# Two attention and MLP layers at one token, 8 rows: key scores of the next row moved ahead of a row's end, norms folded behind the projections, output projection as rows, PSUM banks by purpose

## Chip, cores, metric

One core of one Trainium2 chip runs the whole program. The metric is device time in microseconds (us). "PE" is the tensor engine, "DVE" the vector engine, "ACT" the scalar engine, "POOL" GpSimd, "SP" the engine whose queue issues the loads. PSUM is the memory that PE's products land in, divided into banks; HBM is the main memory that the loads read. The profiler also gives the "granted clock": the share of its full clock that PE was allowed. Rows are counted from 1 in the text.

## The reference, cut to what matters

```python
B, Sq, D = 8, 1, 448;  Hq, Hkv, Sk, Dh = 16, 8, 4096, 256;  F = 1792
def A(x):                        # attention, one query token per row
    q = x @ wq                   # 2 query heads share a key/value head
    p = softmax(q @ k_cache.T * Dh**-0.5)
    return (p @ v_cache) @ wo
def M(x):                        # with one token the shifted half of the mixer is zero
    return x + gelu(layernorm(x) @ w3) @ w4
x = x + A(layernorm(x));  x = x + M(layernorm(x))     # layer 1
x = x + A(layernorm(x));  x = x + M(layernorm(x))     # layer 2, same caches and weights
```

Each row's key or value cache of one head is 2 MB. Both layers read the same caches, so what stays on the chip between a row's layer 1 and its layer 2 need not be loaded twice. Layer 2's queries depend on everything that layer 1 did to that row.

## The kernel before

The kernel holds 30 slots of 512 KB (a quarter of one head's keys or values). Between the layers of a row it keeps the keys of five heads (20 slots) and half of one head's values (2 slots). Three "free heads" keep nothing. A list scheduler written in Python ("the planner") gives every engine a fixed order when the program is built; the loads go through one queue in program order and each waits until its slots are free.

A row ends with a *chain*: x1 (the row after layer 1's attention), a norm, the MLP, x2, a norm, the queries of layer 2, and then the first layer-2 scores. Only those scores free the 20 kept key slots. So from the last layer-1 head until then, the loads have 8 slots to live on.

The chain's norm, cut:

```python
def norm(src, skey, n, second):
    # mean: 4 matmuls with ones;  xc = src - mean;  sq = xc*xc
    pe(mean_mm, 4, ...);  dv(xc ...);  dv(sq ...)
    def var_mm(t):                       # f32 products
        for kc in range(4):
            last = t.matmul(psC[:, 8:8 + n], ones_f[0:k, :], sq[0:k, kc, 0:n], ...)
    pe(var_mm, 16, ...)
    # ... variance, two Newton steps, all on DVE ...
    dv(yb = xc * rstd * mask)            # ahead of the projection

def mlp(src, ...):
    norm(src, skey, n, True)
    pe(h_mm, 56, rd=YB + [...])          # needs yb
    # ... gelu ...
    pe(y_mm, 70, ...)
```

A head, cut. Its scores and its value products share one PSUM bank; two such banks take turns:

```python
def pair(layer, b, h, ...):
    ps, bk = psS[g % 2], ("S", g % 2)
    ks.update(load(A_k_cache, b, h, fresh))
    # per quarter: 8 transposes of 128x128 f32, then 16 score products of 48 columns
    if u not in keep_k: free_slots.append(ks[u])
    # max, exp -> pT, sum
    def back():                          # runs after the next head's scores
        vs.update(load(A_v_cache, b, h, fresh_v))
        # per quarter 8 value products, four column groups; each frees its slot
        # ...
        def wo_mm(t):                    # 20 matmuls per head
            for mt in range(NC5):
                for k in range(4):
                    last = t.matmul(psW[:, mt * YW:(mt + 1) * YW], dup(wo_sb, ...),
                                    bcast(oT[nr][:, c, j:j + 1], YW, 1), ...)
        pe(wo_mm, 20, ...);  dv(acc += psW)
```

The order of the heads:

```python
for b in range(B):
    mid(b, order2[:QFIRST])                    # the chain; QFIRST = 8 query groups
    layer1(b + 1, free_heads[:NFILL])          # NFILL = 2 whole heads beside the chain
    layer2(b, l2_heads[:2])
    layer1(b + 1, free_heads[NFILL:])
    layer2(b, l2_heads[2:])
    layer2(b, free_heads)
    layer1(b + 1, kept_heads)
```

## Time and profile before

| | before |
|---|---|
| median of 3 runs | 1180.18 us (1179.01 to 1184.13) |
| profiled span | 1175.4 us |
| read from HBM | 455.15 MB |
| PE busy | 1002.4 us (85%) |
| x1 to the first layer-2 score | 19.4 us in most rows |

The page of the kernel before, in part: busy time by engine, the rate in 40 equal slices, the instruction queue, HBM bytes, the engines' shares of the chain of work that ended last, and the group of the output projection (busy us, mean ns of one, idle time before it and what ended that).

```profile
span 1175.4 us, 45862 instructions
...
PE 1002.4 (85%) x21205; PEld 858.9 (73%) x21205; DVE 529.1 (45%) x1653; ACT 263.2 (22%) x826; POOL 97.9 (8%) x270
...
GB/s 341 408 420 394 343 415 423 418 402 339 392 422 419 391 374 411 425 415 330 388 423 422 414 354 399 425 418 411 348 396 425 418 396 358 414 413 363 343 424 154
...
q8 instruction: 166, 2.72, 0.9%
...
HBM read 455.15 MB, written 0.01 MB: 387 GB/s over the span
...
PE 61%; DMA 28%; issue 6%; DVE 5%; ACT 0%; POOL 0%; SPq 0%; POOLq 0%
...
L809 PE MATMUL psW<-oT,wo_sb 128*128 128x24 bf16 x2560 | 89.6, 183 | 5.7 <-DVE oT L799 3.3
```

Read the rate line as a heartbeat: the program is bound by its loads at about 420 GB/s, and roughly every fifth slice, once per row, it falls to 330 to 374.

Windows of 5 us around the end of row 2 of the kernel before (columns: busy us of each engine with its instructions, the granted clock, the DMA share, GB/s):

```profile
core 0: us, PE busy (x) PEld busy (x) DVE busy (x) ACT busy (x) POOL busy (x), PEclk, DMA share, GB/s
255.00:260.00 5.00, 4.08 (x34) 3.21 (x33) 1.61 (x4) 0.58 (x1) 0.00 (x0) 0.72 1.03 406
260.00:265.00 5.00, 5.00 (x100) 4.94 (x99) 3.32 (x13) 1.09 (x2) 0.00 (x0) 0.94 0.94 344
265.00:270.00 5.00, 5.00 (x125) 4.97 (x123) 3.47 (x13) 2.40 (x8) 0.75 (x2) 1.00 0.90 299
270.00:275.00 5.00, 5.00 (x142) 4.36 (x139) 2.27 (x8) 0.80 (x2) 0.00 (x0) 1.00 0.75 249
275.00:280.00 5.00, 4.79 (x100) 3.62 (x99) 3.23 (x19) 0.65 (x4) 0.75 (x2) 1.00 0.85 264
280.00:285.00 5.00, 4.29 (x153) 3.83 (x151) 2.03 (x10) 0.65 (x4) 0.75 (x2) 1.00 0.99 397
```

During the dip PE has no idle time left, and DMA does. Who keeps the loads waiting is in the waits of the DMA queue of the kernel before (us waited in total, times, longest):

```profile
SPq L444 <- PE psS L771: 475.2, 148, 11.7
SPq L444 <- PE psS L731: 448.1, 129, 12.3
```

L771 is the value products and L731 the scores: a load waits for PE to be done with the slot. Most of these waits cost nothing, since the queue issues far ahead of the engines that move the data; those at a row's end do.

The timeline of the kernel before, same row (start us, length us, engine, line, what it does):

```profile
260.70 0.17 DVE L821 TENSOR_TENSOR x1T<-acc,psW 128x5 bf16<-128x5 f32 x1
...
262.76 1.12 PE L568 MATMUL psC<-sq,ones_f 128*128 128x1 f32 x8
...
264.70 1.94 PE L838 MATMUL psT<-ident_f,kv 128*128 128x128 f32 x16
...
272.27 2.02 PE L674 MATMUL psC<-hT,w_sb 128*128 128x24 bf16 x70
...
277.89 0.70 PE L809 MATMUL psW<-oT,wo_sb 128*128 128x24 bf16 x20
...
280.26 0.96 PE L731 MATMUL psS<-q2T,kv 128*128 128x48 bf16 x32
```

x1 is there at 260.9 and the first layer-2 score starts at 280.3. In between the chain shares PE with transposes (L838), output projection (L809) and the rest of two whole heads of the next row.

### The profile page before, as it was taken

Reading aid. Unit: us, or ns where it says so; the run is one execution under the profiler, and the core shown is the slowest. Engines: PE = TensorE matmul, PEld = TensorE weight load, DVE = VectorE, ACT = ScalarE, POOL = GpSimd, SP = SyncE. Lnnn points to the kernel's source line nnn. Section 1 sums busy time; section 2 is a strip of 40 time slices with the busy share of each in tenths; the row PEclk is TensorE's granted clock in tenths of the full one; section 3 lists DMA queues with packets and bytes.
Section 4 is the critical chain, followed back from the end, with each engine's and each line's share of the span. In section 5 each row is a group of like instructions: output and inputs, shape, how many; then the busy total and the mean of one; then the engine's idle time right before and its main releaser. Section 6 shows DMA issues by size and latency. Waiting matters only on the chain.

```text
span 1175.4 us, 45862 instructions
## 1 busy us (share of the span) xinstructions
PE 1002.4 (85%) x21205; PEld 858.9 (73%) x21205; DVE 529.1 (45%) x1653; ACT 263.2 (22%) x826; POOL 97.9 (8%) x270
## 2 busy tenths in 40 slices
PE   4886988888898998888878898888978988889887
PEld 4775877777787776777767777776857877677775
DVE  3342534544354533555335543454435543354444
ACT  1221212221222211232122311222112321132111
POOL 0100001001100001000010100000010000110100
PEclk9898979998898988999889998899989998899988
DMA  9999999999999999999999999999999999999993
GB/s 341 408 420 394 343 415 423 418 402 339 392 422 419 391 374 411 425 415 330 388 423 422 414 354 399 425 418 411 348 396 425 418 396 358 414 413 363 343 424 154
DMA packets 62046, 458.10 MB, mean 390 GB/s; under 512 B 6288, under 2 KB 12320, under 8 KB 30240
## 3 DMA queue, kind: packets, MB, share of 16 engines
q1 hardware_dynamic: 61856, 455.19, 95.8%
q8 instruction: 166, 2.72, 0.9%
q14 instruction: 24, 0.20, 0.0%
HBM read 455.15 MB, written 0.01 MB: 387 GB/s over the span
## 4 chain that ended last, share of the span: by engine, by line
PE 61%; DMA 28%; issue 6%; DVE 5%; ACT 0%; POOL 0%; SPq 0%; POOLq 0%
PE psT L838 22%; DMA kv<-in_A_k_cache_dram 17%; PE psS L731 16%; DMA kv<-in_A_v_cache_dram 11%; PE psS L771 9%; PE psW L809 4%; PE psC L628 2%; PE psT L977 2%; DVE oS L783 2%; DVE oS L785 2%; PE psC L568 1%; PE psS L793 1%; PE psC L674 1%; PE psC L650 1%; DVE oT L799 0%
## 5 line engine op out<-in xcount | busy, mean ns | idle before, releaser
L838 PE MATMUL psT<-ident_f,kv 128*128 128x128 f32 x2816 | 390.5, 289 | 9.5 <-DMA kv<-in_A_k_cache_dram 9.2
L846 DVE COPY kv<-psT 128x512 f32<-128x512 f32 x400 | 275.3, 691 | 162.3 <-PE psT L838 158.8
L838 PEld LDWEIGHTS psT<-ident_f,kv 128*128 128x128 f32 x2816 | 326.8, 148 | 22.6 <-DMA kv<-in_A_k_cache_dram 15.6
L847 ACT COPY kv<-psT 128x512 f32<-128x512 f32 x304 | 178.2, 587 | 462.5 <-PE psT L838 462.3
L771 PE MATMUL psS<-kv,pT 128*2 128x256 bf16 x4096 | 173.8, 289 | 37.0 <-DMA kv<-in_A_v_cache_dram 22.3
L752 ACT ACTIVATE pT<-psS,nb 128x32 bf16<-128x32 f32 x256 | 72.9, 295 | 416.9 <-DVE nb L746 416.9
L731 PE MATMUL psS<-q2T,kv 128*128 128x48 bf16 x4096 | 143.0, 190 | 21.3 <-issue 20.3
L731 PEld LDWEIGHTS psS<-q2T,kv 128*128 128x128 bf16 x4096 | 131.3, 101 | 29.1 <-issue 27.7
L731 PE MATMUL psS<-q1T,kv 128*128 128x48 bf16 x4096 | 142.8, 184 | 2.8 <-issue 1.9
L731 PEld LDWEIGHTS psS<-q1T,kv 128*128 128x128 bf16 x4096 | 129.7, 97 | 21.2 <-issue 15.6
L771 PEld LDWEIGHTS psS<-kv,pT 128*2 128x2 bf16 x4096 | 77.7, 85 | 74.9 <-issue 26.5
L744 POOL PARTITION_ALL_REDUCE gm<-pm x128 | 45.4, 355 | 893.2 <-DVE pm L742 770.7
L742 DVE TENSOR_REDUCE pm<-psS 128x2 f32<-128x64 f32 x128 | 28.7, 225 | 156.7 <-PE psS L731 156.1
L809 PEld LDWEIGHTS psW<-oT,wo_sb 128*128 128x128 bf16 x2560 | 80.3, 97 | 21.4 <-DVE oT L799 14.4
L809 PE MATMUL psW<-oT,wo_sb 128*128 128x24 bf16 x2560 | 89.6, 183 | 5.7 <-DVE oT L799 3.3
L783 DVE CAST oS<-psS 128x256 bf16<-128x256 f32 x128 | 54.3, 424 | 87.8 <-PE psS L771 85.0
L793 PEld LDWEIGHTS psS<-sel,oS 128*128 128x128 bf16 x512 | 24.7, 98 | 90.6 <-DVE oS L785 88.6
L793 PE MATMUL psS<-sel,oS 128*128 128x2 bf16 x512 | 32.3, 167 | 67.0 <-DVE oS L785 66.5
L977 PE MATMUL psT<-ident_b 128*128 128x256 bf16 x518 | 85.6, 285 | 1.8 <-issue 1.8
L757 POOL PARTITION_ALL_REDUCE Db<-rs x128 | 51.3, 401 | 154.4 <-ACT pT L752 154.4
L785 DVE TENSOR_TENSOR oS<-psS,oS 128x256 bf16<-128x256 f32 x128 | 54.3, 424 | 2.9
L977 PEld LDWEIGHTS psT<-ident_b 128*128 128x128 bf16 x518 | 40.8, 100 | 16.1 <-issue 12.0
(83 smaller groups left out, 475.4 us busy)
## 6 DMA issues: line engine op xcount, KB each, us to landing
kv<-in_A_v_cache_dram SPq DMA_DIRECT2D x64, 2048.0 KB, 16.6
kv<-in_A_k_cache_dram SPq DMA_DIRECT2D x48, 2048.0 KB, 22.4
kv<-in_A_v_cache_dram SPq DMA_DIRECT2D x86, 1024.0 KB, 19.7
kv<-in_A_k_cache_dram SPq DMA_DIRECT2D x46, 1024.0 KB, 25.6
kv<-in_A_v_cache_dram SPq DMA_DIRECT2D x68, 512.0 KB, 7.4
kv<-in_A_k_cache_dram SPq DMA_DIRECT2D x68, 512.0 KB, 11.6
wo_sb<-in_A_wo_dram SPq DMA_DIRECT2D x1, 3584.0 KB, 46.2
wq_sb<-in_A_wq_dram SPq DMA_DIRECT2D x3, 1024.0 KB, 16.6
```

The costliest lines, as they stand in the source:

```text
L731: last = t.matmul(ps[:, 2 * i:2 * i + 2 * REP], a[:, c:256:2], bcast(rhs(c), REP, 1), start=(c == 0), stop=(c == 1))
L752: return a.activation(pT[nr][:, :, :].rearrange("p i j -> p j i")[:, jj, :], sview[:, jj, :], ACT.Exp, bias=nb[nr][:, jj:jj + 1], scale=IN ...
L757: plan.op("pool", lambda gp: gp.partition_all_reduce(Db[nr][:, :], rs[nr][:, :], P, RO.add), 0.5, "sum", rd=[("rs", nr, 0), ("rs", nr, 1)] ...
L771: last = t.matmul(ps[g4:g4 + 2, PV0:PV0 + DH], pT[nr][:, i, :], slot_ap(q, s * 256, 256), start=(i < 4), stop=(i >= 28), skip_group_check= ...
L783: plan.op("dve", lambda v: v.tensor_copy(oS[:, 0, :], po), 0.36, "o", rd=[("pv", par, x) for x in range(4)], wr=["oS0"], banks=[bk], prio=hi)
L785: plan.op("dve", lambda v: v.tensor_tensor(oS[:, 1, :], po, oS[:, 0, :], ALU.subtract), 0.36, "o", rd=["oS0"] + [("pv", par, x) for x in r ...
L793: last = t.matmul(ps[:, PV1 + 2 * c:PV1 + 2 * c + 2], oS[:, w, c * P:(c + 1) * P], sel[:, :], start=(w == 0), stop=(w == 1))
L809: last = t.matmul(psW[:, mt * YW:(mt + 1) * YW], dup(wo_sb, 2 * (2 * h + j) + c, mt), bcast(oT[nr][:, c, j:j + 1], YW, 1), start=(k == 0), ...
L838: last = t.transpose(psT[bank][:, s * P:(s + 1) * P], src, ident_f[:, :])
L846: return e.tensor_copy(dst, psT[bank][:, :])
L847: return e.copy(dst, psT[bank][:, :])
L977: last = t.matmul(psT[bank][:, 256 * i:256 * i + 256], ident_b[:, :], bcast(ident_b[:, :], 2, 1), start=True, stop=True)
```

## The change

Five things at once. (1) A head is split into a front (keys, scores, exponentials) and a back (values and what follows). The fronts of the next row's three free heads run *ahead* of the row's end, mixed with the kept heads; only their backs stay beside the chain. (2) Norms are folded behind the projections: the raw x goes through the weights while the moments are worked out, and a column sum of the weights corrects the result. (3) The output projection is 4 matmuls of 448 columns per head in four column groups, summed over seven heads in a PSUM bank; then two evacuations and a 10-matmul "turn"; the last head goes directly. (4) PSUM banks by purpose: one for scores, one for values, one for the chain, two for the rows, three instead of four for transposes. (5) The planner models PE's instruction fetches, and a filler (a matmul without use for the result, meant to keep PE's granted clock up) is one product of 512 columns rather than two of 256.

```diff
-LAG = 1
-QFIRST = 8
-NFILL = 2
+AHEAD = 1
+KSTEP = 2
+QFIRST = 1
+NFILL = 3
 ...
-    NT = 4
-    psS = [nc.alloc_psum_tensor(f"psS{i}", [P, 512], f32) for i in range(2)]
-    psC = nc.alloc_psum_tensor("psC", [P, 512], f32)
-    psW = nc.alloc_psum_tensor("psW", [P, 512], f32)
+    NT = 3 if LAY == "A" else 4                        # LAY = "A"
+    psS = nc.alloc_psum_tensor("psS", [P, 512], f32)   # scores
+    psP = nc.alloc_psum_tensor("psP", [P, 512], f32)   # values
+    psR = [nc.alloc_psum_tensor(f"psR{i}", [P, 512], f32) for i in range(2)]
+    psM, M = ...                                       # the chain
 ... mlp:
-        norm(src, skey, n, True)
-        pe(h_mm, 56, rd=YB + [...])
-        dv(hb = psC)
+            sums(src, skey)                            # 4 products of 3 columns
+            moments(True, cs_h, "cs_h", t_h, "t_h")    # DVE, beside the projection
+            pe(lambda t: h_mms(t, lambda kc: src[:, kc, 0:1], ch, 0, 1, HW), 56,
+               rd=[skey] + W3, wr=[kb], banks=[bk])
+            dv(hb = psM * rstd + t_h)
 ... back:
-                for mt in range(NC5):
-                    for k in range(4):
-                        last = t.matmul(psW[...], dup(wo_sb, ...), bcast(oT[...], YW, 1), ...)
-            pe(wo_mm, 20, ...)
+        if k < HKV:
+                for i in range(4):
+                    last = t.matmul(bank[32 * i:32 * i + 1, 0:D], oT[no][:, i % 2, i // 2:i // 2 + 1],
+                                    wo_sb[:, a:a + D], start=(k == 1), stop=(k == HKV - 1),
+                                    skip_group_check=True, tile_position=(0, 32 * i))
+        if k == HKV - 1:   # two evacuations, then the turn of 10 matmuls into acc
+        if k == HKV:       # last head: 20 matmuls, as before
 ... order of the heads:
-        layer1(b + 1, free_heads[:NFILL])
-        layer2(b, l2_heads[:2])
-        layer1(b + 1, free_heads[NFILL:])
-        layer2(b, l2_heads[2:])
-        layer2(b, free_heads)
-        layer1(b + 1, kept_heads)
+        w = [("b", 0, b + 1, h) ... for h in free_heads]     # their backs, beside the chain
+        k = both(1, b, l2_heads)
+        run(w[:NFILL])                                       # ... then k, the kept heads
+            run(both(1, b, free_heads))
+            run(both(0, b + 1, kept_heads, [(0, b + 2, h) for h in free_heads]))
```

## The prediction

> **What bounds the kernel now.** DMA, interrupted once per row by the PE. The page moves 455 MB from HBM, DMA share 96%, mean 390 GB/s. In 5 us windows the undisturbed stretches (60-95 us, 195-250 us) hold 405-434 GB/s, mean near 418; 455.15 MB at 418 is 1089 us, the floor for these bytes. The other 86 us of the span, from the same windows: 6 us at the start, 18 us after the last load, and one dip per row. 260-285 us reads 344, 299, 249, 264, 397 GB/s: 6.4 us lost; 125-150 lost 5.4; 965-1010 about 6; the last row (1070-1115) 9. Eight rows: about 52 us. The rest is scatter.
>
> In those dips the PE is full (260-285: 24.1 of 25 us), and the DMA queue's waits are for PE scores and values (448 and 475 us), that is, for free slots: 20 kept key and 2 kept value slots of 30 leave 8. The timeline of row 2 shows why slots return late: from x1T (260.9) to the first second-layer score (280.3) is 19.4 us. The chain's own PE work (f32 variance 1.12 us twice, hidden layer 1.7, output 2.0, eight query groups at 0.5) competes with two whole heads of the next row, each 3.9 us of transposes, 2.0 scores, 1.1 values, 0.7 wo.
>
> **What the change does, costed.**
> - Keys and scores of three free heads move ahead of the row's end; the chain keeps their values. PE work beside the chain falls from about 15 us to about 5; their 6 MB of values covers 15 us of DMA and waits for nothing in the chain.
> - Norm folded: before, mean to yb took 6.9 us (261.2-268.1) ahead of the hidden layer; now the projection overlaps about 13 DVE operations of 0.2 us: 5.5 us less, and 2 us less before the queries, of which one group, not eight, precedes the first score. Chain: 19.4 to about 12 us (estimate).
> - wo as rows: 20 matmuls (0.69 us) become 4 of 448 columns in four column groups. Value products already use such groups: 16 of 256 columns in 0.61 us, 8 in 0.39; so about 0.37 us (estimate), 112 times: 36 us less PE. The Trainium skill, "TensorEngine Tiling (Array Packing)", Key Properties, says tiles operate independently but changing the mode drains the array; the trace prices that only inside those 0.39 us.
> - Added: column sums once (184 matmuls, about 6 us), two 128x448 evacuations and a 10-matmul turn per row and layer. Transposes get 3 banks, not 4; scores and values one bank each.
>
> About 1,700 fewer matmuls of 21,205.
>
> **Critical path.** Mid-row PE savings are worth nothing: DMA bounds there. The row-end dips are all on it. I expect them to shrink from 6.5 to 1-2 us per row: the new key-heavy stretch (two keys and one value: 14 us of PE per 14.7 us of DMA) is tight. Start and tail stay. 1089 + 6 + 17 + 12 + scatter 6 + 3 (unprofiled against profiled) = 1133 us.
>
> **Predicted:** 1133 us, 1115 to 1158; faster by over 2%: 0.87, within 2%: 0.11, slower: 0.02.
>
> **What would show it.** Mean 402-408 GB/s; windows at row ends above 380; x1 to first second-layer score under 13 us; PE busy 930-960 us; tail near 18 us; bytes unchanged; f32 variance line gone.
>
> **What would make it wrong.** The key-heavy stretch falls behind DMA, so the dip merely moves before the row's end; one score bank makes the next head wait for the exponentials; three banks stall transposes; lower PE load drops the granted clock; small 512 KB loads get more frequent.

## The result, and the profile after

| | before | after |
|---|---|---|
| median | 1180.26 us (1179.01 to 1184.13) | 1149.73 us (1146.58 to 1153.32) |
| ratio, 95% | | 0.9737 (0.9698 to 0.9776): faster |
| profiled span | 1175.4 us | 1144.8 us |
| PE busy, matmuls | 1002.4 us, 21,205 | 970.4 us, 19,393 |
| mean granted clock | 0.927 | 0.927 |

A ratio is the mean time of one kernel's fast runs over that of the other's fast runs of the same rounds, so it is not quite the ratio of the medians quoted.

The page of the kernel after, the lines that answer to those of before:

```profile
span 1144.8 us, 42049 instructions
...
PE 970.4 (85%) x19393; PEld 775.2 (68%) x19393; DVE 544.4 (48%) x1618; ACT 254.6 (22%) x816; POOL 97.9 (9%) x272
...
GB/s 336 407 422 393 390 417 426 419 415 382 419 425 417 395 407 425 425 414 377 409 424 422 417 377 387 424 421 416 383 413 424 418 403 403 411 414 386 420 424 93
...
q8 instruction: 152, 2.49, 0.9%
...
HBM read 455.16 MB, written 0.01 MB: 398 GB/s over the span
...
DMA 58%; PE 34%; DVE 3%; issue 3%; SPq 1%; ACT 1%; POOL 0%
...
L927 PE MATMUL psR<-wo_sb,oT 128*1 128x448 bf16 x448 | 42.7, 369 | 6.4 <-DVE oT L909 5.4
```

The bytes are the same. The heartbeat is still there and much fainter: the low slices now read 377 to 403. The chain of work that ended last was PE for 61% of the span before and is DMA for 58% of it now. The output projection fell from 89.6 us to 42.7 us for the rows, plus 13.2 us for the last heads and 8.9 us for the turns (four more groups of its profile): 64.8 us.

Windows of the kernel after around the end of row 2 (x1 now at 270.7 us):

```profile
core 0: us, PE busy (x) PEld busy (x) DVE busy (x) ACT busy (x) POOL busy (x), PEclk, DMA share, GB/s
255.00:260.00 5.00, 3.87 (x46) 3.32 (x43) 3.73 (x8) 2.32 (x7) 0.76 (x2) 1.00 1.01 406
260.00:265.00 5.00, 3.71 (x105) 2.44 (x105) 1.27 (x5) 0.65 (x4) 0.76 (x2) 1.00 0.78 270
265.00:270.00 5.00, 3.62 (x65) 1.63 (x61) 2.46 (x7) 0.00 (x0) 0.00 (x0) 1.00 1.01 380
270.00:275.00 5.00, 4.58 (x113) 2.79 (x110) 3.22 (x19) 0.00 (x0) 0.00 (x0) 0.69 1.02 412
275.00:280.00 5.00, 5.00 (x123) 3.30 (x122) 1.50 (x10) 0.22 (x1) 0.00 (x0) 0.97 1.03 411
280.00:285.00 5.00, 4.00 (x105) 2.52 (x105) 3.30 (x17) 0.00 (x0) 0.00 (x0) 1.00 1.04 419
```

The chain itself (270 to 285 us) now runs beside full-rate loads. A short dip remains, and it stands *before* x1, at 260 to 265 us. PE isn't full there (3.71 of 5 us): something made it wait.

The timeline of the kernel after, same row; its last line is from row 5, to be used further below (in brackets: the idle time ahead, and what ended it):

```profile
255.38 0.56 PE L831 MATMUL psS<-q1T,kv 128*128 128x48 bf16 x16
...
258.38 0.30 ACT L852 ACTIVATE pT<-psS,nb 128x32 bf16<-128x32 f32 x1
...
260.28 0.61 PE L881 MATMUL psP<-kv,pT 128*2 128x256 bf16 x16 [1.41 <-DMA kv<-in_A_v_cache_dram]
260.82 1.35 PE L831 MATMUL psS<-q1T,kv 128*128 128x48 bf16 x47
...
264.70 0.36 PE L927 MATMUL psR<-wo_sb,oT 128*1 128x448 bf16 x4
...
270.55 0.17 DVE L961 TENSOR_TENSOR x1c<-acc,psM 128x5 bf16<-128x5 f32 x1 [0.85 <-PE psM L788]
...
284.24 1.37 PE L831 MATMUL psS<-q2T,kv 128*128 128x48 bf16 x48
...
702.69 0.72 PE L881 MATMUL psP<-kv,pT 128*2 128x256 bf16 x20 [2.05 <-issue]
```

So the dip arises like this. The last kept head's scores end at 255.9, its exponentials at 258.7. The next scores (the free heads of the row after) use the same bank, so they can't start before. (The Trainium skill, "PSUM — Partial Sum Buffer", section "PSUM bank collisions raise a hardware error", says that two engines may not touch one bank and quadrant at once and that software has to guard it; that is why the planner orders them by bank. No run here shows a collision.) PE then takes values that land at 260.3, and only at 260.8 come the scores that free key slots. The load queue had stood without a free slot from 248.9 to 261.4.

The waits of the DMA queue of the kernel after:

```profile
SPq L481 <- PE psS L831: 479.9, 104, 15.6
SPq L481 <- PE psP L881: 295.9, 122, 10.4
```

The waits for value products shrank by 179 us in total, those for scores did not, and the longest of these grew from 12.3 to 15.6 us. As a sum these waits prove nothing, so I use another measure.

**Lost time.** Every load packet is given the median duration of its size in the trace (161 ns for 4 KB, 313 for 8 KB, 614 for 16 KB), on 16 engines. Time that isn't covered by such work is time that the loads lost. By this, the loads need 1083.9 us at full rate in the kernel before and 1084.9 us after: the floor. For each of the eight rows I add up what was lost in four stretches: from 18 to 2 us ahead of x1 ("before x1"), from there to the first layer-2 score ("chain"), in the 30 us after that, and in the rest of the row. The table has the sums over the rows, the mean time from x1 to the first layer-2 score, and the tail from the last load's landing to the end. About 7 us are lost from the start to 18 us ahead of the first x1 in all kernels but one (e5).

| | median us | before x1 | chain | 30 us after | rest | x1 to score | tail |
|---|---|---|---|---|---|---|---|
| before | 1180.3 | 0.4 | 37.3 | 23.0 | 5.3 | 18.8 | 16.9 |
| after | 1149.7 | 15.4 | 2.7 | 7.4 | 5.1 | 13.7 | 20.2 |
| e1, two score banks | 1148.4 | 3.6 | 9.1 | 11.1 | 5.1 | 13.3 | 21.8 |
| e2, keys in the chain | 1177.6 | 0.3 | 52.1 | 6.6 | 4.8 | 18.3 | 18.6 |
| e3, serial norm | 1161.3 | 18.5 | 4.5 | 21.1 | 5.1 | 16.1 | 17.8 |
| e4, wo as tiles | 1168.8 | 15.2 | 7.8 | 19.3 | 6.0 | 15.5 | 20.9 |
| e5, 4 transpose banks | 1162.0 | 17.1 | 4.5 | 7.0 | 5.4 | 13.8 | 18.9 |
| e6, planner's loads 5% slower | 1153.3 | 14.0 | 6.7 | 12.8 | 5.2 | 13.5 | 19.3 |
| e7, filler in pairs | 1152.8 | 18.6 | 5.5 | 9.2 | 5.4 | 13.7 | 21.5 |
| e9, AHEAD = 2 | 1154.1 | 0.6 | 9.3 | 27.9 | 5.1 | 14.1 | 17.8 |
| e11, no values kept | 1158.5 | 13.3 | 2.6 | 3.3 | 5.1 | 14.0 | 18.3 |
| e12, banks shared as before | 1144.6 | 4.6 | 8.1 | 16.6 | 5.1 | 13.9 | 19.3 |
| e13, wider scores | 1171.2 | 29.8 | 3.7 | 13.6 | 5.6 | 13.7 | 21.6 |
| e14, order alone | 1169.2 | 15.1 | 6.7 | 22.1 | 6.1 | 17.0 | 23.0 |

The first three columns, the row ends, went from 60.7 to 25.5 us. Together with a tail that is 3.3 us longer this is 31.9 us, against 30.6 us between the two spans: that is where the time came from. One profile is one run, and the runs of one kernel differ by 2 to 9 us, those of the kernel before by up to 13.5. e6 and e7, which took the same time as the kernel after to within 4 us, lost 33.5 and 33.3 us at the row ends against its 25.5, so differences of up to 8 us in these columns are not to be explained. (The profile of the kernel after is of its fastest run, 1146.58 us, that of e12 of its slowest, 1148.31 us.)

### The profile page after: what moved, and what is told of

Its sections match the earlier page's. It is cut to its first block, busy times and chain, and to the rows that moved or that the text cites. A ratio compares the mean times of both kernels' runs of the same rounds, so it can differ in the third digit from the quotient of the medians.

```text
span 1144.8 us, 42049 instructions
## 1 busy us (share of the span) xinstructions
PE 970.4 (85%) x19393; PEld 775.2 (68%) x19393; DVE 544.4 (48%) x1618; ACT 254.6 (22%) x816; POOL 97.9 (9%) x272
## 4 chain that ended last, share of the span: by engine, by line
DMA 58%; PE 34%; DVE 3%; issue 3%; SPq 1%; ACT 1%; POOL 0%
DMA kv<-in_A_k_cache_dram 29%; DMA kv<-in_A_v_cache_dram 28%; PE psT L978 12%; PE psS L831 10%; PE psP L881 5%; PE psM L691 2%; PE psT L1135 1%; SPq L481 1%; PE psR L927 1%; PE psM L705 1%; PE psM L785 1%; PE psP L903 1%; DVE oS L893 1%; DVE oS L895 1%; PE psM L788 1%
## 5 line engine op out<-in xcount | busy, mean ns | idle before, releaser
L881 PE MATMUL psP<-kv,pT 128*2 128x256 bf16 x4096 | 163.9, 288 | 36.7 <-DMA kv<-in_A_v_cache_dram 27.5
L831 PE MATMUL psS<-q2T,kv 128*128 128x48 bf16 x4096 | 136.4, 188 | 17.1 <-issue 14.8
L881 PEld LDWEIGHTS psP<-kv,pT 128*2 128x2 bf16 x4096 | 81.5, 85 | 83.2 <-DMA kv<-in_A_v_cache_dram 42.5
L842 DVE TENSOR_REDUCE pm<-psS 128x2 f32<-128x64 f32 x128 | 28.6, 224 | 134.6 <-PE psS L831 131.5
L893 DVE CAST oS<-psP 128x256 bf16<-128x256 f32 x128 | 54.3, 424 | 63.4 <-PE psP L881 58.8
L1135 PE MATMUL psT<-ident_b 128*128 128x512 bf16 x234 | 79.8, 430 | 0.0
L903 PEld LDWEIGHTS psP<-sel,oS 128*128 128x128 bf16 x512 | 24.6, 98 | 65.7 <-DVE oS L895 60.7
L903 PE MATMUL psP<-sel,oS 128*128 128x2 bf16 x512 | 32.1, 166 | 42.1 <-DVE oS L895 40.6
L895 DVE TENSOR_TENSOR oS<-psP,oS 128x256 bf16<-128x256 f32 x128 | 54.3, 424 | 3.1
L852 ACT ACTIVATION_READ_ACCUMULATOR pT<-psS,nb 128x1 f32 x256 | 50.9, 199 | 0.0
L927 PE MATMUL psR<-wo_sb,oT 128*1 128x448 bf16 x448 | 42.7, 369 | 6.4 <-DVE oT L909 5.4
L691 PEld LDWEIGHTS psM<-x2c,wq_sb 128*128 128x128 bf16 x768 | 29.8, 98 | 22.9 <-issue 12.0
## 6 DMA issues: line engine op xcount, KB each, us to landing
kv<-in_A_v_cache_dram SPq DMA_DIRECT2D x72, 1024.0 KB, 13.6
wq_sb<-in_A_wq_dram SPq DMA_DIRECT2D x3, 1024.0 KB, 16.8
```

Of the source, the lines that this page charges most:

```text
L691: last = t.matmul(bank[:, at + i * step:at + i * step + copies], w, r, start=(kc == 0), stop=(kc == 3))
L831: last = t.matmul(ps[:, 2 * i:2 * i + 2 * REP], a[:, c:256:2], bcast(rhs(c), REP, 1), start=(c == 0), stop=(c == 1))
L852: return a.activation(pT[nr][:, :, :].rearrange("p i j -> p j i")[:, jj, :], sview[:, jj, :], ACT.Exp, bias=nb[nm][:, jj:jj + 1], scale=IN ...
L881: last = t.matmul(ps[g4:g4 + 2, PV0:PV0 + DH], pT[nr][:, i, :], slot_ap(q, s * 256, 256), start=(i < 4), stop=(i >= 28), skip_group_check= ...
L893: plan.op("dve", lambda v: v.tensor_copy(oS[:, 0, :], po), 0.36, "o", rd=[("pv", par, x) for x in range(4)], wr=["oS0"], banks=[bk], prio=hi)
L895: plan.op("dve", lambda v: v.tensor_tensor(oS[:, 1, :], po, oS[:, 0, :], ALU.subtract), 0.36, "o", rd=["oS0"] + [("pv", par, x) for x in r ...
```

## The experiments

Four groups of runs, each group with its own runs of the kernel before (medians 1180.52, 1183.56, 1180.89 and 1180.97 us; the second is that of e5, e6, e7 and e9). The kernel after was not run again in these groups, so "slower than the kernel after" compares medians of different groups, and a few us there are not shown. All results were correct. Letters in the quoted expectations stand for theories. A is mine: what is left at a row's end is the turnaround of slots, held up by the one score bank, and PE's work elsewhere is free. Its rivals, each tied to one part, are spelled out in the texts.

### e1: two score banks

```diff
+    l0 = [0]
-        par, nr, nm = 0, g % NR, g % 3
-        ps, bk = psS, "S"
+        par = 0
+        if layer == 0:
+            par = l0[0] % 2
+            l0[0] += 1
+        ps, bk = ((psS, "S"), (psM, M))[par]      # unused columns of the chain's bank
```

> The kernel after, with the first-layer scores in two banks in turn (the second in unused columns of the chain's bank). Theory A (the dip left at each row's end comes from the one score bank: in row 2 the scores of the last key fetched ahead could not start before the exponentials of head 7 were done at 258.8 us, and its four slots came free at 261.4 to 262.6, after the queue had run dry): the dips shrink from about 3.5 to 1-2 us a row, 12 to 16 us less than the kernel after, 1133 to 1139 us, ratio to before 0.960 to 0.965. Rival B (with 20 key slots held, 8 to 10 slots and the landing time bound it, whatever the bank): within 4 us of the kernel after, ratio 0.970 to 0.977.

Measured: 1148.35 us, ratio to before 0.9713 (0.9658 to 0.9768), which is the kernel after's time. The dip did go: before x1 the loss fell from 15.4 to 3.6 us. It came back: 6.4 us more in the chain, 3.7 us more after it. Windows of e1, end of row 2:

```profile
260.00:265.00 5.00, 2.98 (x77) 1.50 (x72) 2.70 (x9) 0.65 (x4) 0.75 (x2) 1.00 1.02 394
265.00:270.00 5.00, 3.63 (x53) 1.76 (x53) 1.41 (x5) 0.00 (x0) 0.00 (x0) 0.60 1.01 394
270.00:275.00 5.00, 5.00 (x100) 2.67 (x98) 3.45 (x21) 0.00 (x0) 0.00 (x0) 0.50 1.02 397
275.00:280.00 5.00, 5.00 (x133) 3.68 (x131) 2.12 (x13) 0.21 (x1) 0.00 (x0) 0.88 0.88 351
280.00:285.00 5.00, 3.82 (x119) 2.83 (x120) 2.64 (x11) 0.00 (x0) 0.00 (x0) 1.00 0.91 315
```

The 270 GB/s at 260 us are gone, and 351 and 315 stand at 275 and 280 us instead. PE was idle 2 us at 260 and 1.4 us at 265, and was granted 0.60 and 0.50 of its clock in the windows from 265 us on, just as the chain began. That is row 2 alone: over the eight rows the clock granted between x1 and the first layer-2 score, read from the traces row by row, is 0.87 in e1 and 0.86 in the kernel after (1.00 in the kernel before), so a colder clock is not what gave e1's gain back. The Trainium skill, "TensorE: Matmul & The Clock Gate", section "What's actually happening", says that the throttled clock is the default and that activity releases it; these windows agree. So the score bank explains where the dip stands, not what the row's end costs. The gain was given back later in the row. One reservation: the second score bank is the chain's, though the chain got no longer (13.3 us for 13.7).

### e2: the lighter kernel with the order of before

```diff
-    run(both(0, 0, kept_heads[1:], [(0, 1, h) for h in free_heads]))
+    lagged(0, 0, kept_heads[1:]);  settle()
     for b in range(B):
         mid(b, order2[:QFIRST])
-        ...                                  # backs beside the chain, fronts ahead
+        lagged(0, b + 1, free_heads[:2])
+        lagged(1, b, l2_heads[:2])
+        lagged(0, b + 1, free_heads[2:])
+        lagged(1, b, l2_heads[2:])
+        lagged(1, b, free_heads)
+        lagged(0, b + 1, kept_heads)
+        settle()
```

> The kernel after, with the heads in the order of the kernel before: keys and scores of the next row's free heads stay in the chain; all else of the change stays. Theory A (the move ahead is what paid): most of the gain is lost, ratio 0.99 to 1.00, row-end dips of 5 us and more. Rival B (the shorter chain and the lighter PE paid): most of the gain stays, ratio 0.975 to 0.985, dips about 4 us.

Measured: 1177.64 us, ratio 0.9965 (0.9911 to 1.0018): the gain is gone. 52.1 us are lost in the chains, more than before the change. Windows of e2 at the end of row 2:

```profile
265.00:270.00 5.00, 5.00 (x134) 4.91 (x132) 2.73 (x9) 1.45 (x7) 0.75 (x2) 1.00 0.78 297
270.00:275.00 5.00, 4.39 (x126) 3.71 (x122) 3.82 (x18) 1.06 (x2) 0.02 (x1) 1.00 0.55 175
```

The dip of before is back, deeper. Folded norms and cheap output rows on their own bring 0.35%, not clear of zero. One reservation: e2 has the banks of after, one for all scores, with the order of before, and I did not build that order with shared banks. If these banks hold that order back, part of what is put down to the order here is theirs.

### e3: the projections wait for the moments

```diff
-               rd=[skey] + W3, wr=[kb], banks=[bk])
+               rd=[skey, "t_h"] + W3, wr=[kb], banks=[bk])
-                           1, QW), 16, rd=[("x2", b)] + WQ, ...
+                           1, QW), 16, rd=[("x2", b), "t_q"] + WQ, ...
```

> The kernel after, with the hidden layer and the queries waiting for the folded norm's moments, so that nothing overlaps them. Theory A (the values of three heads cover the chain, so its length is off the critical path): at most 5 us slower than the kernel after, ratio 0.972 to 0.978. Rival B (the chain's length is what the DMA queue waits for): about 2 to 2.5 us more per row, ratio 0.986 to 0.992.

Measured: 1161.25 us, ratio 0.9820 (0.9768 to 0.9873), 11.5 us slower than the kernel after and between the two theories' figures. The chain got 2.4 us longer (13.7 to 16.1), and three quarters of the added loss stand in the 30 us after it (7.4 to 21.1). With the cheap projection, the chain's length is not covered by the values that are loaded beside it.

### e4: the output projection as 20 matmuls for every head

```diff
-        if k < HKV: ... wo_row ...          # 4 matmuls of 448 columns
-        if k == HKV - 1: ... turn ...
+        def wo_mm(t):
+            for mt in range(NC5):
+                for i in range(4):
+                    last = dup(t, psR[0], YC + mt * YW, YW, wo_sb, (4 * h + i) * D, mt, ...)
+        pe(wo_mm, 20, ...);  dv(acc += psR[0])
```

> The kernel after, with wo as 20 matmuls for every head (in a bank of its own) in place of rows of 4. PE busy rises by about 35 us. Theory A (PE time in mid-row is free): at most 6 us slower than the kernel after, ratio 0.972 to 0.979. Rival B (PE instructions count wherever they are, by fetching them or by holding slots): 15 us or more slower, ratio 0.985 or more.

Measured: 1168.84 us, ratio 0.9896 (0.9832 to 0.9960), 19 us slower than the kernel after. The PE line of its page, and one of the two groups of its projection:

```profile
PE 1008.9 (87%) x20992; PEld 831.3 (71%) x20992; DVE 545.8 (47%) x1692; ACT 249.4 (21%) x806; POOL 98.0 (8%) x272
...
L785 PE MATMUL psR<-oT,wo_sb 128*128 128x12 bf16 x1536 | 61.2, 174 | 7.8 <-issue 3.5
```

38.5 us more PE time than the kernel after's 970.4. My statement that such savings are worth nothing falls here. The table shows where they count: in the rest of the row the loss rose by 0.9 us only, but by 5.1 us in the chain and 11.9 us after it. Two reservations. The other 1,024 products of this projection have 64 columns of weights and take 42.8 us by the same profile, 104.0 us in all: this is dearer than the 89.6 us of the kernel before, so e4 undoes more than the change did. And its chains ran at a granted clock of 0.70, for 0.86 in the kernel after; how much of the 19 us that makes is open, but e12 below had 0.71 there and was not slower than the kernel after.

### e5: the fourth transpose bank back

```diff
-    LAY = "A"
+    LAY = "C"        # the chain shares the score bank, which gives a bank to the transposes
```

> The kernel after with its other layout of banks: the chain's products share the bank of the scores, and the transposes get a fourth bank back. Theory A (what is left per row is set by the time from the last key's scores to the first second-layer score, on the PE's order of work): sharing makes the chain wait for scores and the other way round, 0 to 10 us slower than the kernel after, ratio 0.974 to 0.983. Rival C (three transpose banks are what holds the key-heavy stretch back): 8 us or more faster, ratio 0.967 or less.

Measured: 1162.04 us, ratio 0.9828 (0.9800 to 0.9856), 12 us slower. But not in the row ends, which lost 28.6 us against 25.5. The extra time stands in the first row. Windows of e5:

```profile
100.00:110.00 10.00, 7.47 (x193) 6.25 (x197) 0.73 (x4) 0.65 (x4) 0.75 (x2) 0.83 0.21 76
110.00:120.00 10.00, 7.29 (x212) 5.17 (x211) 3.40 (x14) 1.94 (x12) 2.13 (x6) 1.00 0.64 216
```

Here the column sums of the weights, which now stand in the scores' bank, wait for a weight load (PE stands 2.8 us for it; in the kernel after it stands 2.0 us for the same load, but in the chain's own bank), and the scores wait behind them; that this makes up all of the loss is argued and was not tested. The kernel after has 385 and 417 GB/s in these two stretches. From the start to the first row's end 19.3 us are lost instead of 6.8. What this run can tell: a fourth transpose bank that is paid for with a shared bank wins nothing at the row ends, so rival C gets no support. It doesn't tell what four banks would do without the shared bank.

### e6: the planner's loads as slow as measured

```diff
-    FASTER = 1.05
+    FASTER = 1.0
```

> The kernel after, with the planner's DMA 5% slower, near the measured rate. Rival D (the PE's fixed order was planned for a DMA faster than it is, so the PE stands in line behind value products whose data has not landed while scores that would free slots wait): the PE's waits for values fall and the time falls by 5 us or more, ratio 0.969 or less. Theory A (order is not it): within 4 us, ratio 0.970 to 0.977.

Measured: 1153.34 us, ratio 0.9750 (0.9720 to 0.9779): the same as the kernel after. A 5% slower DMA in the planner changes nothing that can be seen; rival D gets no support.

### e7: fillers as two matmuls of 256 columns

```diff
-            return t.matmul(psT[bank][:, :], ident_b[:, :], bcast(ident_b[:, :], 4, 1), ...)
+            for i in range(2):
+                last = t.matmul(psT[bank][:, 256 * i:256 * i + 256], ident_b[:, :],
+                                bcast(ident_b[:, :], 2, 1), start=True, stop=True)
```

> The kernel after, with each clock-keeping product split in two of half the width, as in the kernel before: same order, same columns, about 234 more pairs for the PE to fetch. Rival E (fetching PE instructions is what costs at the row's end, which would also explain the 19 us of the wo tiles): 4 us or more slower, ratio 0.977 or more. Theory A: within 3 us, ratio 0.971 to 0.976.

Measured: 1152.77 us, ratio 0.9746 (0.9717 to 0.9774) with 234 more matmuls: within 3 us of the kernel after, so no effect that this run can see. Rival E, that the number of PE instructions to be fetched costs the time, gets no support. Alone this does not refute it for e4, which has 1,599 more matmuls and not 234: 3 us for 234 would be 20 us for those (an estimate in proportion).

It wasn't a foolish rival. In the kernel after all 26 PE stalls of over 0.7 us that the trace calls "issue" (35.5 us in all; the line at 702.69 us above is one) hold or adjoin a 16 KB packet on the instruction queue, and PE resumes 1.2 to 1.6 us after it. In the kernel before all 25 such stalls (43.2 us) do. But e4, 19 us slower than the kernel after, has 37.6 us of such stalls, hardly more than the kernel after's 35.5. See also e13.

### e9: fronts ahead earlier

```diff
-AHEAD = 1
+AHEAD = 2
```

> The kernel after, with the three free heads' keys fetched earlier among the kept heads' (the last of them before head 7's values and not last of all). Theory A (idle DMA time per row is the time from the last key slots freed to the first second-layer scores, less what the free slots can take in): an earlier last key does not shorten it; the dip moves, total within 5 us of the kernel after, ratio 0.970 to 0.978. Rival F (the dip is the late scores of the last key alone): 8 us or more faster, ratio 0.967 or less.

Measured: 1154.10 us, ratio 0.9759 (0.9724 to 0.9794). The loss before x1 fell from 15.4 to 0.6 us, and that in the 30 us after rose from 7.4 to 27.9 us. As in e1, the dip moves and does not go. Rival F falls.

### e11: two more slots, at the price of 8.4 MB

```diff
-KEEP_V = 2
+KEEP_V = 0
```

> The kernel after with no values kept, so ten slots and not eight are free at the row's end, for eight times 1 MB more to load (8.4 MB, 20 us at 418 GB/s). Theory A (idle DMA per row is what the free slots cannot take in during that interval, two slots more are 2.4 us of DMA): lost DMA time at the row ends falls from about 25 us to under 12, so the kernel is only 5 to 13 us slower than the kernel after, ratio 0.977 to 0.986. Rival H (slots are not what binds there): lost time stays near 25 us, the kernel is 18 us or more slower, ratio 0.988 or more.

Measured: 1158.50 us, ratio 0.9810 (0.9786 to 0.9833), reading 463.54 MB. The time came out as theory A expected, but not for its reason. 8.4 MB more at 418 GB/s are about 20 us (an estimate from the rate between dips), and the run is 8.8 us slower than the kernel after: some 11 us better than its bytes ask for. The row ends lost 19.2 us instead of 25.5, where A had asked for under 12. Free slots count, but only for part of the loss.

### e12: scores and values of a head share a bank, as before the change

```diff
-PV0 = 0
+PV0 = 128
-        ps, bk = psS, "S"                                # front
+        ps, bk = ((psS, "S"), (psP, "P"))[g % 2]
-        ps, bk = psP, "P"                                # back
+        ps, bk = ((psS, "S"), (psP, "P"))[g % 2]
```

> The kernel after with the banks of the kernel before for scores and values: two banks, each with the scores of one head and the value products of one head, used in turn, in place of one bank for scores and one for values. Everything else stays. Theory A (the interval from the last key's scores to the first second-layer score decides, whatever the bank): within 5 us of the kernel after, ratio 0.970 to 0.978. Rival G (single banks hold the chain: the next head's values wait for the previous head's sums to leave the one value bank): the interval falls from 22.5 us and the time by 6 us or more, ratio 0.968 or less.

Measured: 1144.55 us, ratio 0.9689 (0.9662 to 0.9716). Banks by purpose, which the change introduced, gain nothing that this run shows with this order. Nominally this is the fastest kernel of all, 5 us under the kernel after. The two were measured in different groups and their intervals overlap, so that it beats the kernel after is not shown; that it beats the kernel before is. Again the dip before x1 nearly goes (15.4 to 4.6) and the loss after the chain grows (7.4 to 16.6).

Theory A had a number of its own, the time from the last key score of layer 1 to the first of layer 2, in which no key slot comes free: 22.5 us in the kernel after, 21.6 in e1, 24.9 in e3, 23.9 in e4 (means of the first six rows). The row-end losses of these four follow it, but not those of e12 and e13 (24.2 and 22.1 us, for 29.3 and 47.1 us lost at row ends). That interval alone is not the cause.

### e13: wider score products, the same number of them

```diff
-REP = 24        # a score product has 2 * REP columns
+REP = 40
```

> The kernel after with 40 copies and not 24 of the queries in each score product: same number of PE instructions, wider products (80 columns for 48). It separates PE time from PE instructions as the reason for the 19 us of the wo tiles. If PE time counts (the scores of kept heads after the chain are what frees slots): PE busy up by 20 us or more and 8 us or more slower than the kernel after, ratio 0.980 or more. If the number of instructions counts: within 5 us, ratio 0.970 to 0.978.

Measured: 1171.21 us, ratio 0.9929 (0.9893 to 0.9964), 21 us slower than the kernel after. The PE line of its page:

```profile
PE 1036.0 (89%) x19374; PEld 851.4 (73%) x19374; DVE 539.9 (46%) x1612; ACT 258.2 (22%) x822; POOL 97.9 (8%) x272
```

65.6 us more PE time with 19 fewer matmuls. The "issue" stalls of over 0.7 us *fell* from 35.5 to 13.2 us while the time rose. So PE's time costs without any more instructions; that their number costs besides, no run shows. And the loss is again at the row ends: before x1 it doubled (15.4 to 29.8), in the rest of the row it rose by 0.5 us.

### e14: the new order alone

The edits of e3 and e4 together: the order of after, with the long chain and the dear output projection.

```diff
+  rd=[skey, "t_h"] + W3   and   rd=[("x2", b), "t_q"] + WQ      # as e3
+  wo_mm of 20 matmuls for every head                            # as e4
```

> The kernel after with both lightenings of the row's end undone (wo as 20 matmuls for every head, hidden layer and queries waiting for the moments): what is left is the order of heads, the banks and the smaller norm. Undoing them one at a time cost 19 and 11 us. Theory J (the order needs the lighter PE: moving the keys makes the stretch before the row's end PE-bound, and only the PE time saved there pays for it): the costs add up or nearly, 1170 to 1182 us, ratio 0.990 to 1.001, so the order alone gains nothing as the lightening alone (keys in the chain, 0.9965) gained nothing. Rival K (the two undone parts cost the same idle time, once): 1163 to 1170 us, ratio 0.985 to 0.990.

Measured, over five rounds: 1169.21 us, ratio 0.9908 (0.9876 to 0.9941). This is e4's time; the long chain costs nothing more that this run can see once the projection is dear (the time is in rival K's range, the ratio at the low end of theory J's). With e2 it completes a square, though not a clean one: e14 and e2 have the banks, the smaller norm and the planner of after, and e14's projection, like e4's, is dearer than that of before (103.3 us for 89.6 by their profiles).

| ratio to before | long chain, dear projection | short chain, cheap projection |
|---|---|---|
| order of before | 1 | 0.9965 (e2) |
| order of after | 0.9908 (e14) | 0.9737 (after) |

The order without lightness brings 0.9%, lightness without the order 0.35%, both together 2.6%: more than the sum. The dearer projection makes the 0.9% too small: 13.7 us more PE time at e4's rate (19 us for 38.5) are about 7 us or 0.6% (an estimate). That leaves some 0.8% above the sum, hardly more than the intervals allow, so that the parts together beat their sum is likely and not shown by the times. The lost time points the same way. At the row ends 60.7 us (before), 43.9 (e14), 59.0 (e2), 25.5 (after).

## Why the prediction was right or wrong

The verdict was right (faster by over 2%), and 1149.7 us lies within 1115 to 1158. The gain was 2.6% where 4% was named, so 17 us are to be accounted for.

- **"The floor for these bytes", 1089 us.** Right. The bytes are unchanged and the packets add up to 1084.9 us.
- **"About 1,700 fewer matmuls"; output row "about 0.37 us".** Right: 1,812 fewer, and 0.36 us for the four matmuls of 448 columns in the timeline at 264.70 us. (The Trainium skill, "TensorEngine Tiling (Array Packing)", Key Properties, says that changing the tiling mode drains the array; no run here isolates what that takes.) PE busy 970.4 us, a little above the 930 to 960 named.
- **"Chain: 19.4 to about 12 us".** Nearly: 13.7 us on the mean.
- **Mechanism: the dips at the row ends are on the critical path and shrink when the keys move ahead.** Right: without the new order 0.35% is left (e2, which has the banks of after), and e14 has the order bring 0.9% without the lighter PE work.
- **Mis-sized term: "I expect them to shrink from 6.5 to 1-2 us per row", 12 us in the sum.** They shrank to 3.2 us per row (from 7.6 by the same measure), 25.5 us in all: 13.5 of the 17 us. Another 3 us is the tail, 20.2 us where the sum had 17. That the tail got longer I haven't explained. The rest of the sum stands within 4 us each way.
- **"Windows at row ends above 380".** Wrong: 270 GB/s at 260 to 265 us. The listed risk that "the dip merely moves before the row's end" came true, by way of the one score bank, another listed risk. But mending that bank (e1, e12) or running fronts earlier (e9) only moved the idle time once more. Three transpose banks are no cause that e5 shows. The risk that the granted clock drops came true where the mean hides it: the mean is 0.927 in both profiles, but between x1 and the first layer-2 score it fell from 1.00 to 0.86 (means of eight rows). "Lower PE load", as the prediction put it, does not explain it alone, since e4 had more PE work and 0.70 there. What the drop costs no run isolates; e12 had 0.71 and took no longer than the kernel after.
- **Wrong step: "Mid-row PE savings are worth nothing: DMA bounds there."** The second half holds: the rest of the row lost 5.1 us with the cheap projection, 6.0 with the dear one (e4) and 5.6 with the wide scores (e13). The first half does not follow, because the savings were not mid-row. They fall on every head, and the stretch in which the losses stand is long: from 18 us ahead of x1 to 30 us after the first layer-2 score are 62 us of a row's 136. For e4, 62/136 of its 38.5 us extra PE time is 17.5 us, an estimate that takes the work as evenly spread; its row-end losses rose by 16.8 us. For e13 the same estimate gives 30 us, and they rose by 21.6 us. The even spread is rough: the traces have 24 us (e4) and 19 us (e13) more PE busy time in these stretches than the kernel after's 404 us. I had costed the 36 us of projection saved in rows (25 us net of the turns and of dearer last heads) at zero, while the predicted 1-2 us per row silently relied on it: e14, without it and with the long chain, loses 5.5 us per row.

What stays open. How the remaining loss at a row's end divides between PE's time and the turnaround of slots: e13 and e4 show the first to count, e11 shows two more slots to be worth some 11 us of time (6.3 of the 25.5 us in the table), and no run separates them wholly, since PE's work is what frees slots. How much of e4's and e14's loss comes from the colder clock in their chains (0.70 and 0.66). Whether shared banks (e12) really beat the kernel after. Why the tail is 3 us longer.

## What to carry to other kernels

When a dip moves but does not shrink as you remove the wait it stood at, the wait was only where a shortage showed; look at how much work the engine must do in the whole stretch, not at the last wait. "Off the critical path" must be asked of each stretch of time and not of each kind of work: an operation that every head does is partly on it. A granted clock is also to be read by stretch: the mean of 0.927 was the same before and after while that of the chains fell from 1.00 to 0.86. And parts of a change that each bring little alone (0.35% and, with a projection dearer than before, 0.9% here) can be worth 2.6% together when they relieve the same stretch, so judge them by undoing one at a time from the finished kernel as well as by doing one alone.

## What the Trainium skill lacked or had wrong

- "Runtime: NRT & Kernel Launch", "Instruction fetch mechanics", gives the size of an instruction fetch, but no page that I found gives a time that PE loses to one. Here the instruction queue moved 166 packets of 16 KB for 21,205 matmuls and 152 for 19,393 (one for each 128 load and matmul pairs, by these counts), and PE's stalls of up to 3.1 us before and 2.3 us after end 1.2 to 1.6 us after such a packet. Yet e13 had fewer of these stalls (13.2 us against 35.5) and was 21 us slower.
- "TensorEngine Tiling (Array Packing)", Key Properties, says that changing the mode drains the array, and gives no time for it. Here four products of 448 columns in four column groups take 0.36 us together; a drain is not isolated.
- "DMA: Bandwidth & Descriptors", Measured, has 341 GB/s for a transfer of 1 MB; its table is for SWDGE transfers issued from GpSimd. For the queued loads here that would be too low: by the median packet, loads of 512 KB in rows of 4 KB run at 407 GB/s, and rows of 8 and 16 KB (loads of 1 and 2 MB) at 419 and 427 (estimates from 161, 313 and 614 ns per packet on 16 engines).
- "TensorE: Matmul & The Clock Gate", "What's actually happening", is right as far as these runs show (0.60 and 0.50 granted in e1 during and after 10 us with 3.4 us of idle time). What the runs add: the mean over a run can hide a colder clock in the stretch that matters, 0.86 in the chains of the kernel after for 1.00 before with 0.927 over both runs, and PE's total busy time does not foretell it (0.70 in e4, with 38.5 us more).
